# The inverse root of the query and key norms: one power on GpSimd in place of logarithm, exponential and three Newton operations

## The chip, the cores and the metric

The kernel runs on one core of a Trainium2 chip. The metric is device time in microseconds of one execution. Three runs of the kernel before gave 1486.89, 1487.9 and 1488.19 us; the median is 1487.9.

The core has five engines that work side by side, each through its own queue of instructions in order: TensorE (PE; its weight loads are shown apart as PEld), VectorE (DVE), ScalarE (ACT), GpSimd (POOL) and SyncE (SP, which here only starts DMA transfers). An instruction that waits holds everything behind it on its engine.

## The reference, cut to what matters

An attention block whose queries and keys are normalised, then a feed-forward block with a gate. The shapes: 8 batches, 12 heads, 448 tokens, 64 numbers a head; the feed-forward block has 3584 tokens, 768 inputs, 1536 hidden units.

```python
def rmsnorm(x, g):
    rms = np.sqrt(np.mean(x * x, axis=-1, keepdims=True) + 1e-06)
    return x / rms * g
q_n, k_n = (rmsnorm(q, g_q), rmsnorm(k, g_k))
scores = (1 / np.sqrt(64)) * np.matmul(q_n, k_n.transpose(0, 1, 3, 2))
attn = softmax(scores)                     # row by row
x = heads_side_by_side(np.matmul(attn, v)) # 3584 x 768
g = x @ w_gate
out = (g / (1 + np.exp(-g)) * (x @ w_val)) @ w_out
```

The change touches one thing in it: how `1 / sqrt(sum of squares + 64e-6)` is computed for each token and head of q and k. The factor sqrt(64) that turns the mean into a sum is folded into the gains.

## The kernel before, in words

The kernel holds two paths: `fast`, which ran here, and `general`, which is taken only where the gains are large and didn't run.

**Pairs.** Attention is done for two heads of one batch at a time, 48 such pairs in all. `attention(m)` adds the pieces of pair m: queries and keys come in by DMA as blocks of 32 x 32 (L728); ScalarE squares them (L754), VectorE sums the squares of each 32 numbers (L768), ScalarE copies the half sums to the partitions of the neighbouring half (L778), and VectorE adds the two halves and the small constant (L782). Then comes the inverse root (L678 to L686, below). GpSimd multiplies the keys and then the queries by it (L795), VectorE transposes both (L811), ScalarE scales the queries by the gains (L814), and TensorE makes the scores (L840). Exponentials follow on ScalarE (L855), the weighted sums on TensorE (L916), the denominators on TensorE (L947), a reciprocal on VectorE (L982), and the division (L1005, L1008, L1012).

**Inverse root.** `inverse_root` adds two pieces. The first, on ScalarE, is `rr = exp(-0.5 * ln(ss * GAIN**-2))`, two instructions on a tile of 128 x 28. It needs the table set that holds logarithm and exponential, which the planner calls mode "logarithms". The second, on VectorE, is a Newton step of three instructions on tiles of the same size. The result is larger than the true inverse root by the factor GAIN; the gains are multiplied by GAIN**-2 to take the two factors (of queries and keys) out again.

**Stages.** Twelve pairs (batches 0 and 1) are done first, while weights are loaded and converted: each of 24 parts is fetched by DMA, scaled on ScalarE (L1146, L1150), rounded on VectorE (L1168, L1174, L1180), combined on GpSimd in twelve sums (L1199, L1202), and stored back to DRAM, all as a preparation of a faster form of matrix product. Then come four blocks, each of two batches. A block has an up phase (gate and value products, L1328, with Silu on ScalarE, L1402) and a down phase (L1502). Beside the down phase of blocks 0 to 2 run the twelve attention pairs of the next two batches. Silu needs another table set than the exponential, so ScalarE loads a table (L552 and L1402 in the trace) each time it goes from one to the other.

**What sets the order.** Nothing runs in the order in which the text has it. `Order` is a planner: each piece is added with its engine, an expected time in us, a due time, the pieces it follows, the buffers it takes and uses, and a mode. `run` plays all pieces through a model of the engines, and emits at each step the piece that can start first, with ties broken by due time; a piece on GpSimd is handicapped by 0.7 us in that choice, and a change of table set on ScalarE counts 1.3 us. Pieces with `port=True` are kept from overlapping with each other between VectorE and GpSimd. `takes` names a buffer out of a ring; a piece that takes one waits for the last user of the old content. The planner's times only set the order: on the chip each instruction waits by semaphores for what it needs.

The planner's entries for the inverse root are 0.5 us on ScalarE and 0.45 us on VectorE; the buffer ring `rr` has four places, `ss` two.

Of the kernel before, what the change touches and what calls it, by code (L numbers as in the profile page):

```python
# [9 lines left out]
F32 = mybir.dt.float32  # L10
U32 = mybir.dt.uint32
I64 = mybir.dt.int64
AF = mybir.ActivationFunctionType
ALU = mybir.AluOpType
# [346 lines left out]
class Order:  # L361
# [24 lines left out]
    def add(  # L386
        self, engine, us, when, emit, after=(), takes=(), uses=(), port=False, kb=0, group=None,
        mode=None, early=None, rank=0.0, slack=0.1,
    ):
        piece = dict(  # L390
            engine=engine, us=us, when=when, emit=emit, takes=takes, port=port, kb=kb,
            group=group, mode=mode, early=early, rank=rank, slack=slack,
            after=[a for a in after if a is not None], end=None, n=len(self.pieces),
        )
        for tile_of in (*takes, *uses):
            self.users.setdefault(tile_of, []).append(piece)
        self.pieces.append(piece)
        return piece
# [79 lines left out]
def fast(  # L478
# [41 lines left out]
    nc = tc.nc  # L520
# [3 lines left out]
    P = 128  # L524
# [15 lines left out]
    const = ctx.enter_context(tc.tile_pool(name="const", bufs=1))  # L540
# [7 lines left out]
        rr=4, ws=2, **{x + str(i): 1 for x in "vw" for i in range(6)},  # L548
# [5 lines left out]
    order = Order(BUFS, dict(logarithms=load_tables))  # L554
    tiles = {}
# [10 lines left out]
    def take(name, key, shape):  # L566
        if name in ("e", "ea"):
            at = order.turn[name] % BUFS[name]
            tiles[name, key] = es[:, at] if at < BUFS["e"] else more_es[:, at - BUFS["e"]]
            return tiles[name, key]  # L570
        if name in OFTEN:
            at = OFTEN[name] + order.turn[name] % BUFS[name]
            tiles[name, key] = spare[:, ts(at, S)]
            return tiles[name, key]
        if name == "eh":
            at = order.turn["eh"] % BUFS["eh"]
            tiles[name, key] = more[:, at].rearrange("p (h q) -> p h q", h=2)
            return tiles[name, key]
        if name in WORK:
            at, size = WORK[name]  # L580
            at += order.turn[name] % BUFS[name] * size
            n = 1
            for length in shape[1:]:
                n *= length
            x = work[0 : shape[0], at : at + n]
            letters = "abcd"[: len(shape) - 1]
            x = x.rearrange(
                f"p ({' '.join(letters)}) -> p {' '.join(letters)}",
                **dict(zip(letters, shape[1:])),
            )  # L590
            tiles[name, key] = x
            return x
        pool = psum if name in ("st", "at") else sbuf
        tiles[name, key] = pool.tile(shape, F32, name=name, bufs=BUFS[name])
        return tiles[name, key]
# [33 lines left out]
    gq2 = const.tile([P, 1], F32, name="gq2")  # L629
    gk2 = const.tile([P, 1], F32, name="gk2")  # L630
    gg = const.tile([P, 1], F32, name="gg")

# [14 lines left out]
    def pair_time(m):  # L649
        if m < EARLY:  # L650
            return LEAD + m * PAIR, PAIR
        n, i = divmod(m - EARLY, EARLY)
        return block_end(n) + (i - 1) * BOTH / EARLY, BOTH / EARLY
# [10 lines left out]
    down_products = {}  # L664


    GAIN = 2.0**24

    SCALE = 2.0**8
    SPREAD = 6.0  # L670

    def inverse_root(m, sums, of, when, rank=0.0):


        def estimate():
            ss = of()
            rr = take("rr", m, list(ss.shape))
            nc.scalar.activation(rr, ss, AF.Ln, scale=GAIN**-2)  # L678
            nc.scalar.activation(rr, rr, AF.Exp, scale=-0.5)

        def improve():
            ss, rr = of(), tiles["rr", m]
            times = nc.vector.scalar_tensor_tensor
            times(ss, rr, GAIN**-2, ss, op0=ALU.mult, op1=ALU.mult)  # L684
            times(ss, ss, -0.5, rr, op0=ALU.mult, op1=ALU.mult)
            times(rr, ss, 1.5, rr, op0=ALU.add, op1=ALU.mult)  # L686

        first = order.add(
            "ACT", 0.5, when, estimate, after=[sums], uses=[("ss", m)], takes=[("rr", m)],
            mode="logarithms", rank=rank,  # L690
        )
        return order.add(
            "DVE", 0.45, when + 1.0, improve, after=[first], uses=[("ss", m), ("rr", m)],
            rank=rank,
        )

    NC = S // C
    clusters = {}
# [4 lines left out]
    def attention(m):  # L703
# [10 lines left out]
        ready = base - span  # L714
        early = m < EARLY
        rank = 60.0 if early else 0.0

        def add(*what, **more):
            return order.add(*what, rank=rank, **more)
# [37 lines left out]
        for x in range(2):  # L757
# [3 lines left out]
                    after=[loaded[x], *squares], uses=[("qk", (m, x))] + [("t", m)] * x,  # L761
                    takes=[("t", m)] * (1 - x),
# [17 lines left out]
        def both():  # L780
# [5 lines left out]
        sums = add(  # L786
            "DVE", 1.1, ready - 17.0, summed, after=squares, uses=[("t", m)], takes=[("ss", m)]
        )
        sums = add("ACT", 0.9, ready - 16.0, swap, after=[sums], uses=[("ss", m)])
        sums = add("DVE", 0.15, ready - 15.0, both, after=[sums], uses=[("ss", m)])  # L790
        rr = inverse_root(m, sums, lambda: tiles["ss", m][:, 0], ready - 14.0, rank)

        def scale(x):
            rr = tiles["rr", m][:, ts(x, NC)].rearrange("p (c one) -> p c one", one=1)
# [8 lines left out]
                uses=[("qk", (m, x)), ("t", m), ("rr", m)],  # L803
# [9 lines left out]
        def queries():  # L813
# [7 lines left out]
            uses=[("t", m)],  # L821
# [3 lines left out]
            uses=[("t", m), ("qk", (m, 0))],  # L825
# [3 lines left out]
            takes=[("QT", m)],  # L829
# [19 lines left out]
        def weights_of(j):  # L849
            return ("ea" if early else "e", (m, j)) if j < NJ - 1 else ("eh", m)  # L850
# [20 lines left out]
        for j in (3, 0, 1, 2):  # L871
            before = clusters.get((m - 2, "weighted" if j in (3, 0) else "total"))
            when = (ready + 0.3 if j in (3, 0) else base) + 0.01 * (j % 3)
# [3 lines left out]
                after=[kt, qt, staged.get(ES), before],  # L877
                uses=[("KT", m), ("QT", m)], takes=[("st", (m, j))],
# [4 lines left out]
                after=[st], uses=[("st", (m, j))],  # L883
                takes=[weights_of(j)], mode="logarithms",
            )
            if j in (1, 2) and not early:

                def more_sums(j=j):
                    if j == 1:
# [7 lines left out]
                        takes=[("sums", m)] if j == 1 else [],  # L897
# [57 lines left out]
        when = base + span * 0.8 if late else pair_time(m + 1)[0] + 0.1  # L955
        at = [("at", (m, x)) for x in range(2)]
        last = None
        for j in range(NJ):
# [3 lines left out]
                after=[*ex.values(), load_v, last, clusters.get((m - 1, "total"))],  # L962
                takes=at if j == 0 else [],
                uses=[weights_of(j), ("v", m)] + at * (j > 0),
# [6 lines left out]
            after=[last, *adds] + ([bank_read[m % 2]] if of_bank else []),  # L971
            uses=[weights_of(j) for j in range(NJ)] if early else [("sums", m)],
            takes=[] if of_bank else [den], group=("c", m + 1), mode="strips",
# [36 lines left out]
        def divide():  # L1010
# [9 lines left out]
            takes=[("rd", m)],  # L1020
        )
        if early:
            inv = add(
                "PE", 0.82, when + SPREAD, spread_by_product, after=[inv], mode="full", slack=1.0,
                uses=[("rd", m)] + ([] if of_bank else [den]),
            )
        else:
            inv = add(
                "ACT", 3.0, when + 4.5, spread, after=[inv, staged.get(SPARE)], uses=[("rd", m)],
                takes=[("inv", m)],  # L1030
# [3 lines left out]
            uses=([] if of_bank else [den]) if early else [("inv", m)], port=not early,  # L1034
# [554 lines left out]


    nc.gpsimd.memset(many, SCALE)
    nc.gpsimd.memset(halves, 0.0)
    for x in range(2):
        nc.gpsimd.memset(halves[ds(D * x, D), x], SCALE)
# [7 lines left out]
    for i in range(P // C):  # L1602
# [2 lines left out]
    gains = order.add(  # L1605
        "DVE", 0.2, 9.0,
        lambda: nc.vector.scalar_tensor_tensor(
            out=gg, in0=gq2, scalar=8.0 * GAIN**-2, in1=gk2, op0=ALU.mult, op1=ALU.mult
        ),
        early=0.0,  # L1610
    )
    for m in range(EARLY):
        attention(m)
    first = [(up_weights, i) for i in range(4 * NG)] + [(down_weights, i) for i in range(2 * NG)]
# [11 lines left out]
    for n in range(NB):  # L1626
        block(n)
        for m in range(EARLY * (n + 1), min(NM, EARLY * (n + 2))):
            attention(m)
# [4 lines left out]
def kernel(  # L1634
# [27 lines left out]
    )  # L1662
    nc.vector.tensor_scalar(out=fits, in0=top, scalar1=8.0, scalar2=None, op0=ALU.is_le)
    fast(tc, *args)
    fits = nc.values_load(fits[0:1, 0:1], min_val=0, max_val=1)
    with tc.If(fits == 0):
# [31 lines left out]
```

## Time and profile before

| what | value |
|---|---|
| median of three runs | 1487.9 us |
| span of the profiled execution (first to last instruction) | 1484.0 us |
| median less that span | 3.9 us |
| mean granted TensorE clock | 0.997 |
| scaling on GpSimd (L795), 96 instructions | 105.9 us, mean 1122 ns, median 941 ns |
| logarithm (L678) and exponential (L679) on ScalarE, 48 each | 10.7 us, 224 ns and 10.9 us, 226 ns |
| Newton step on VectorE (L684, L685, L686), 48 each | 12.0 us, 250 ns; 9.0 us, 187 ns; 10.8 us, 224 ns |
| sum of the two halves on VectorE (L782), 48 | 18.7 us, mean 389 ns, median 186 ns, longest 2083 ns |
| table loads on ScalarE | 22 of 1283 ns |

The last instructions of the profile are output transfers; the span runs from the first to the last instruction, and what lies around it (start and end of the execution) is in the time of a run, but not in the span. The profile has no time of its own for the whole execution: the profiled execution is known by its span alone, and the runs by their times.

A line of the profile names the line of the program, the engine, the operation, the tile it writes and the tiles it reads, and then the shape. Two instructions of one line with different tiles are two groups. A bracket such as `[0.55 <-ACT rr L679]` says that the engine had been idle for 0.55 us and that the end of the named instruction let it go on.

### The profile page before, as it was taken

Reading aid. Unit: us, or ns where it says so; the run is one execution under the profiler, and the core shown is the slowest. Engines: PE = TensorE matmul, PEld = TensorE weight load, DVE = VectorE, ACT = ScalarE, POOL = GpSimd, SP = SyncE. Lnnn points to the kernel's source line nnn. Section 1 sums busy time; section 2 is a strip of 40 time slices with the busy share of each in tenths; the row PEclk is TensorE's granted clock in tenths of the full one; section 3 lists DMA queues with packets and bytes.
Section 4 is the critical chain, followed back from the end, with each engine's and each line's share of the span. In section 5 each row is a group of like instructions: output and inputs, shape, how many; then the busy total and the mean of one; then the engine's idle time right before and its main releaser. Section 6 shows DMA issues by size and latency. Waiting matters only on the chain.

```text
span 1484.0 us, 19470 instructions
## 1 busy us (share of the span) xinstructions
PE 1425.0 (96%) x6672; PEld 675.4 (46%) x6672; DVE 916.0 (62%) x1405; ACT 681.5 (46%) x1366; POOL 414.1 (28%) x468
## 2 busy tenths in 40 slices
PE   5789999999999999999999999999999999999998
PEld 2334544443444455544444445554444445555553
DVE  4777887877978544355886733454786854432533
ACT  6774544437775322445767422354676532122100
POOL 2454586636444100012544200011343410000000
PEclk9999999999999999999999999999999999999999
DMA  7767999974453432533344432352353442222235
GB/s 165 158 144 236 292 308 341 296 219 90 99 115 85 113 106 71 138 103 90 74 111 110 100 117 73 106 136 77 96 119 85 90 119 89 80 98 73 83 98 107
DMA packets 415921, 193.30 MB, mean 130 GB/s; under 512 B 324164, under 2 KB 397892, under 8 KB 409668
## 3 DMA queue, kind: packets, MB, share of 16 engines
q1 hardware_dynamic: 402688, 190.35, 48.0%
q10 hardware_dynamic: 12996, 1.61, 0.7%
q8 instruction: 55, 0.90, 0.3%
q14 instruction: 54, 0.44, 0.1%
q0 software_dynamic: 128, 0.00, 0.0%
HBM read 157.29 MB, written 34.60 MB: 129 GB/s over the span
## 4 chain that ended last, share of the span: by engine, by line
PE 73%; DVE 3%; ACT 2%; issue 1%; DMA 1%; SPq 1%; ACTq 0%; DVEq 0%
PE mm L1502 22%; PE mm L1328 20%; PE at L1328 20%; PE st L840 6%; PE at L916 5%; PE st L947 1%; ACT spare L1000 1%; ACT es L855 1%; DVE rd L982 1%; DMA out_dram<-spare 0%; SPq L728 0%; DVE ss L782 0%; DMA work<-in_k_dram 0%; DVE ss L768 0%; DVE sums L866 0%
## 5 line engine op out<-in xcount | busy, mean ns | idle before, releaser
L1328 PE MATMUL mm<-xs,ws 128*128 128x448 f32 x960 | 401.2, 540 | 4.4 <-DVE spare L1276 2.2
L1328 PE MATMUL at<-xs,ws 128*128 128x448 f32 x960 | 400.6, 540 | 4.1 <-DVE v L1274 2.6
L1328 PEld LDWEIGHTS mm<-xs,ws 128*128 128x128 f32 x960 | 181.5, 190 | 185.8 <-issue 173.8
L1328 PEld LDWEIGHTS at<-xs,ws 128*128 128x128 f32 x960 | 181.9, 190 | 184.6 <-issue 172.6
L795 POOL TENSOR_TENSOR work<-work,rr 128x448 f32<-128x448 f32 x96 | 105.9, 1122 | 503.5 <-DVE rr L686 245.2
L840 PE MATMUL st<-work 64*64 64x448 f32 (+1 forms) x1536 | 155.1, 508 | 27.3 <-ACT work L814 21.2
L1502 PE MATMUL mm<-gt,ws 128*128 128x448 f32 x448 | 177.2, 545 | 0.0
L1272 DVE TENSOR_TENSOR gt<-gt,mm 128x448 f32<-128x448 f32 x64 | 39.7, 621 | 185.1 <-PE mm L1328 171.3
L1502 PE MATMUL mm<-hs,ws 128*128 128x448 f32 x384 | 152.1, 545 | 0.9 <-DVE ss L684 0.9
L855 ACT ACTIVATE es<-st 128x896 f32<-128x896 f32 x129 | 114.3, 913 | 56.1 <-PE at L916 42.8
L860 POOL TENSOR_TENSOR sums<-es 128x896 f32<-128x896 f32 x36 | 75.7, 2104 | 195.8 <-PE st L947 83.2
L1402 ACT ACTIVATE st<-gt 128x448 f32<-128x448 f32 x96 | 52.4, 547 | 163.8 <-DVE gt L1276 85.9
L1000 ACT COPY spare<-rd 32x224 f32<-32x224 f32 x288 | 108.1, 375 | 35.0 <-DVE rd L982 30.7
L1502 PEld LDWEIGHTS mm<-gt,ws 128*128 128x128 f32 x448 | 82.9, 190 | 84.2 <-issue 81.0
L916 PE MATMUL at<-es,v 64*64 64x448 f32 x1032 | 110.2, 545 | 7.2 <-ACT xs L1005 3.3
L1270 ACT COPY gt<-mm 128x448 f32<-128x448 f32 x80 | 42.5, 531 | 141.5 <-PE mm L1328 141.4
L1502 PEld LDWEIGHTS mm<-hs,ws 128*128 128x128 f32 x384 | 71.1, 190 | 72.9 <-issue 70.9
L840 PEld LDWEIGHTS st<-work 64*64 64x64 f32 x1536 | 50.9, 134 | 108.7 <-issue 38.1
L1270 ACT COPY v<-at 128x448 f32<-128x448 f32 x96 | 51.1, 532 | 83.2 <-PE at L1328 80.0
L860 POOL TENSOR_TENSOR sums<-sums,es 128x896 f32<-128x896 f32 x36 | 78.7, 2187 | 2.8
L811 DVE STREAM_TRANSPOSE work<-work 128x448 f32<-128x448 f32 x96 | 59.2, 627 | 25.2 <-POOL work L795 23.1
L916 PEld LDWEIGHTS at<-es,v 64*64 64x64 f32 x1032 | 39.7, 134 | 67.4 <-issue 57.4
(150 smaller groups left out, 1568.7 us busy)
## 6 DMA issues: line engine op xcount, KB each, us to landing
ws<-up_sides SPq DMA_DIRECT2D x32, 1024.0 KB, 4.9
ws<-down_sides SPq DMA_DIRECT2D x16, 1024.0 KB, 5.0
ws<-down_sides SPq DMA_DIRECT2D x28, 512.0 KB, 4.0
ws<-up_sides SPq DMA_DIRECT2D x16, 768.0 KB, 4.6
work<-in_q_dram SPq DMA_DIRECT2D x192, 56.0 KB, 2.4
work<-in_k_dram SPq DMA_DIRECT2D x188, 56.0 KB, 2.5
out_dram<-spare SPq DMA_DIRECT2D x168, 56.0 KB, 1.9
v<-in_v_dram SPq DMA_DIRECT2D x96, 96.0 KB, 2.5
```

The lines of the kernel that those rows point to most:

```text
L795: nc.gpsimd.tensor_tensor(out=tiles["t", m][:, x], in0=tiles["qk", (m, x)], in1=rr.to_broadcast([P, NC, C]), op=ALU.mult,)
L811: nc.vector.transpose(to, tiles["t", m][:, x].rearrange("p c f -> p (c f)"))
L840: nc.tensor.matmul(st[ds(D * x, D), h, 0:n], tiles["KT", m][rows, ds(P * j + D * of_keys, D)], tiles["QT", m][rows, ds(Q * of_queries, n)] ...
L855: nc.scalar.activation(e, tiles["st", (m, j)][:, :, 0 : S * width(j) // P], AF.Exp)
L860: nc.gpsimd.tensor_tensor(out=to, in0=tiles["e", (m, 0)] if j == 1 else to, in1=e, op=ALU.add)
L916: nc.tensor.matmul(tiles["at", (m, x)][ds(D * h, D), queries], tiles["v", m][rows, j, h], tiles["e", (m, j)][rows, h], start=j == 0, stop= ...
L1000: nc.scalar.copy(inv[ds(D * h + C * to, C), ts(x, Q)], tiles["rd", m][ds(D * h + C * x, C)])
L1270: nc.scalar.copy(to, ps)
L1272: nc.vector.tensor_tensor(out=to, in0=old, in1=ps, op=ALU.add)
L1328: nc.tensor.matmul(ps(), w[:, at, which, c], xs[:, SLOT[x], c], start=fresh and c == 0, stop=c == NC2 - 1, skip_group_check=True,)
L1402: nc.scalar.activation(take(*act, [P, 2, TB])[:, 0, 0:S], to, AF.Silu)
L1502: nc.tensor.matmul(banks[s][:, 0:S], w[:, at, s, g], where[x][:, g], start=fresh and g == 0, stop=g == NG - 1, skip_group_check=True,)
```

## The change

`inverse_root` and its two pieces go, and GAIN with them. In their place `attention` adds one piece on GpSimd: the sum raised to the power minus one half, on the same 128 x 28 tile, with the exponent read from a column of -0.5 that is spread along the row. That column is filled once at the start by a memset on GpSimd. The new piece has a planner time of 0.5 us and the due time of the old first piece, is not marked `port`, and has no table mode. The gains lose the factor GAIN**-2. The table set that is loaded for exponentials stays the same, under the same name.

```diff
+    minus_half = const.tile([P, 1], F32, name="minus_half")
...
-    GAIN = 2.0**24
...
-    def inverse_root(m, sums, of, when, rank=0.0):
-        def estimate():
-            ss = of()
-            rr = take("rr", m, list(ss.shape))
-            nc.scalar.activation(rr, ss, AF.Ln, scale=GAIN**-2)
-            nc.scalar.activation(rr, rr, AF.Exp, scale=-0.5)
-
-        def improve():
-            ss, rr = of(), tiles["rr", m]
-            times = nc.vector.scalar_tensor_tensor
-            times(ss, rr, GAIN**-2, ss, op0=ALU.mult, op1=ALU.mult)
-            times(ss, ss, -0.5, rr, op0=ALU.mult, op1=ALU.mult)
-            times(rr, ss, 1.5, rr, op0=ALU.add, op1=ALU.mult)
-
-        first = order.add(
-            "ACT", 0.5, when, estimate, after=[sums], uses=[("ss", m)], takes=[("rr", m)],
-            mode="logarithms", rank=rank,
-        )
-        return order.add(
-            "DVE", 0.45, when + 1.0, improve, after=[first], uses=[("ss", m), ("rr", m)],
-            rank=rank,
-        )
...
-        rr = inverse_root(m, sums, lambda: tiles["ss", m][:, 0], ready - 14.0, rank)
+
+        def roots():
+            nc.gpsimd.tensor_tensor(
+                out=take("rr", m, [P, 2 * NC]), in0=tiles["ss", m][:, 0],
+                in1=minus_half.to_broadcast([P, 2 * NC]), op=ALU.pow,
+            )
+
+        rr = add(
+            "POOL", 0.5, ready - 14.0, roots, after=[sums], uses=[("ss", m)], takes=[("rr", m)]
+        )
...
+    nc.gpsimd.memset(minus_half, -0.5)
...
-            out=gg, in0=gq2, scalar=8.0 * GAIN**-2, in1=gk2, op0=ALU.mult, op1=ALU.mult
+            out=gg, in0=gq2, scalar=8.0, in1=gk2, op0=ALU.mult, op1=ALU.mult
```

## The prediction

> **What bounds the kernel now.** I read the page first (busy shares, then the forty slices), then busy time by stretch, then TensorE's waits in the first 140 us, then the first 15 us instruction by instruction, because the stretches point there.
>
> ```profile
> PE 1425.0 (96%) x6672; PEld 675.4 (46%) x6672; DVE 916.0 (62%) x1405; ACT 681.5 (46%) x1366; POOL 414.1 (28%) x468
> ...
> PE   5789999999999999999999999999999999999998
> ```
>
> TensorE is busy for 1425.0 of 1484.0 us: 59.0 us are all that any change off TensorE can win. The second line says that the holes lie in the first four slices. By stretch (columns: stretch, its length, PE, PEld, DVE, ACT, POOL busy, clock, DMA share, GB/s):
>
> ```profile
> 0.00:20.00 20.00, 5.34 (x40) 1.98 (x40) 7.47 (x23) 9.18 (x22) 6.56 (x16) 1.00 0.76 146
> ...
> 40.00:60.00 20.00, 14.28 (x181) 5.95 (x179) 13.93 (x27) 13.78 (x28) 7.30 (x12) 1.00 0.68 167
> 60.00:80.00 20.00, 16.30 (x172) 6.83 (x168) 17.73 (x29) 16.77 (x33) 13.79 (x21) 1.00 0.81 190
> ...
> 140.00:320.00 180.00, 173.62 (x461) 86.54 (x460) 145.86 (x218) 81.00 (x109) 112.42 (x218) 1.00 0.98 302
> 320.00:505.00 185.00, 179.73 (x1131) 76.56 (x1129) 146.89 (x217) 119.93 (x277) 81.27 (x48) 1.00 0.46 104
> 505.00:690.00 185.00, 184.94 (x527) 92.41 (x528) 81.95 (x146) 63.81 (x122) 11.93 (x10) 1.00 0.36 102
> ```
>
> The seven stretches up to 140 us hold 105.6 us of TensorE work, so 34.4 us are idle; from 140 to 505 us 11.7; from 505 to 1400 only 5.5; in the tail from 1400 7.4. In the up phase of block 1 (505 to 690) 0.06 us are idle: nothing can be won there. What TensorE waits for up to 140 us (total us, times, longest):
>
> ```profile
> PE st L840 <- ACT work L814: 21.2, 6, 14.7
> PE at L916 <- ACT xs L1005: 3.3, 2, 2.3
> PE at L916 <- DVE xs L1008: 2.7, 2, 2.1
> PE at L916 <- ACT gt L855: 2.3, 2, 1.3
> PE mm L990 <- DVE rd L982: 2.0, 2, 1.3
> ```
>
> 14.7 of the 21.2 us are the start; the other five waits for the scaled queries (L814) hold 6.5 us. The start, in order of time (start, length, engine, line):
>
> ```profile
> 9.80 0.19 DVE L782 SCALAR_TENSOR_TENSOR ss<-ss 128x28 f32<-128x28 f32 x1 [0.95 <-ACT ss L778]
> ...
> 10.02 0.23 ACT L678 ACTIVATE rr<-ss 128x28 f32<-128x28 f32 x1 [0.25 <-DVE ss L782]
> 10.28 0.23 ACT L679 ACTIVATE rr<-rr 128x28 f32<-128x28 f32 x1
> ...
> 10.98 0.19 DVE L686 SCALAR_TENSOR_TENSOR rr<-ss,rr 128x28 f32<-128x28 f32 x1
> ...
> 11.39 1.83 POOL L795 TENSOR_TENSOR work<-work,rr 128x448 f32<-128x448 f32 x2 [7.79 <-DMA v<-in_v_dram]
> ```
>
> So from the end of the sum (9.99) to the first scaling on GpSimd (11.39) pass 1.40 us, and every one of them delays the first matmul at 14.66.
>
> **What the Trainium skill says.** GPSIMD Engine Reference, section 7, gives 4 cycles per element for a dependent fp32 chain, and section 1 a clock of 1.2 GHz; no page prices a power, and no power runs in this trace. SBUF — State Buffer, "Who interferes with whom": a VectorE instruction with two SBUF inputs and a GpSimd instruction that reads SBUF exclude each other, the later one blocks. The trace agrees: the last Newton operation (L686) has a median of 188 ns and a maximum of 1956, the scaling (L795) a median of 941 and a maximum of 2815. ScalarE: Activation LUTs, "What ACT_TABLE_LOAD costs", says about 1283 ns; the trace has 22 loads of 1283 ns.
>
> **Removed.** ScalarE: 48 × (224 + 226) ns = 21.6 us, of it 5.3 us in the first 140. VectorE: 48 × (250 + 187 + 224) ns = 31.8 us, 6.8 of it in the first 140. Table loads: in the up phases of blocks 1 and 2 five return trips (at 613, 640, 962, 976 and 996 us) load the exponential's set directly before a logarithm. Exponentials that follow at 659 us would load it anyway, so I count three to five trips gone, 6 to 10 loads, 7.7 to 12.8 us of ScalarE. All of that lies under TensorE at 184.94 of 185 us: worth nothing. The constant in the gains and one memset (about 0.1 us, before GpSimd's four short gain loads, 8 us ahead of its first use): nothing.
>
> **Added.** 48 powers on 128x28. Floor: plain sums on GpSimd take about 0.47 us on 128x128 and 0.73 on 128x256, so 2.0 ns an element and 0.21 us fixed: 0.27 us on 28. From above: with c dependent operations an element, 28 × 4 / 1.2 ns = 0.093 us each (estimate from the skill's section 7); the power replaces a logarithm and an exponential, and I take c between nothing and 30: 0.3 to 3.1 us. I take c = 15: 0.27 + 1.4 = 1.7 us. The planner believes 0.5.
>
> **Moved.** The old way from sum to scaling, read off the first seven pairs: 1.40, 1.80, 1.31, 2.36, 2.03, 1.64, 1.43 us, mean 1.71. The new way: a semaphore's 0.22 us (L686's end at 11.17 to 11.39) plus the power; the scaling follows on the same engine. Break-even is a power of 1.2 us for the first pair and 1.5 for the mean one.
> Behind the waiting power stand, on GpSimd's queue, the two scalings of its pair and the conversion's sums (L1199, L1202), for which the store of the weights' sides on SP's queue waits; later the sums of exponentials (L860), for which the denominators wait. In blocks 1 to 3 a pair has 28.3 us and GpSimd needs about 6.3 of them, so 1.7 more hide. That cover would be gone only from some 20 us a power.
>
> **Sum.** First pair: 0.22 + 1.7 − 1.40 = +0.5. The five later waits on L814, each longer by 0.22 + 1.7 − 1.71 = 0.2: +1.0. VectorE's queue up to 140 us: its transposes (L811) stand at the head waiting for GpSimd (24 waits in the run, 23.1 us). The planner errs by 1.7 − 0.5 = 1.2 us a pair where it erred by about 0.2 (0.45 for three operations that need 0.66), so 12 × 1.0 = 12 us more of such waits, against 6.8 us of work and some 3 to 4 us of waits for L679 taken away: 1 to 2 us net, say +1. Block 0's second half (5.3 us idle) and its edges: +0.5. Together +3 on the span of 1484.0, so 1487. The median of the runs stands 3.9 us above that span (1487.9), so 1491.
>
> **Rivals.**
> A short power. At 0.5 us the first pair gains 0.7, the five waits 1.0 each, and VectorE's relief takes a fraction of the 4.7 us that TensorE waits for L1008 and L982: −5, 1483. For it: the removed pieces are on the path in the only stage with room. Against it: at 44 and 58 us the queries waited behind squares (L754) whose loads were late, and a shorter root moves no DMA. It decides from a power below 0.8 us.
> A long power, 3 us: the first pair +1.8, the five waits +1.5 each, VectorE's extra waits 12 × 2.5 − 10 = 20, of which half hides: +15 with the overlap taken off, 1503. For it: no operation in this trace says that it is cheap.
> GpSimd late with the weights: its queue loses 12 × 1.2 = 14 us against the plan while it forms the weights' sides. From 140 to 320 us the DMA engines are at 0.98, so sides stored late aren't caught up, and the products of block 0 wait. If half of it arrives, +7 to +10: 1497. Against it: GpSimd stands idle for 6 to 16 of every 20 us before 140.
> No effect: the new wait ends within 0.5 us of the old one and other queues decide: 1488. That the power isn't computed where the change says can't be: it is one instruction on a named engine; only its price is open.
>
> **How the numbers follow.** What this kernel's measurement tells from no change is 0.2%, 3.0 us: faster is under 1484.9, slower over 1490.9. The forecast (1486 to 1496) has 0.45, of which 0.30 lies above 1490.9 and 0.15 within; the short power 0.18 (0.17 faster, 0.01 within); the long power 0.14; GpSimd late 0.14; no effect 0.09 within. Faster 0.17, within 0.25, slower 0.58. The range 1483 to 1506 leaves out the faster half of the short power (0.09) and the powers beyond 3.1 us (0.07); the forecast's own range is 1486 to 1496.
>
> **What would show it.** The power's mean length on GpSimd, 1.7 us. The first scaling at 11.9 and the first matmul at 15.2 us. No logarithm, 12 to 16 table loads. TensorE's idle time before 140 us at 36 to 38 instead of 34.4, and the stretches after 505 us within 1 us. It is wrong if the power takes under 0.8 or over 3 us, or if the loss or the gain lies after 505 us: then the emitted order, not the length of the chain, made it.

## The result, and the profile after

The changed kernel takes 1596.61 us (median of 4 runs, 1596.06 to 1597.97) against 1487.39 us beside it: 1.0739 times as long, 95% interval 1.0724 to 1.0754. The prediction of 1491 us, and its range up to 1506, are far below it. The page of the changed kernel, busy shares and the first lines of the slices and groups:

```profile
span 1594.7 us, 19324 instructions
...
PE 1468.6 (92%) x6672; PEld 688.4 (43%) x6672; DVE 896.1 (56%) x1261; ACT 657.3 (41%) x1264; POOL 644.1 (40%) x517
...
PE   4787889996888899999998999999998989999998
...
PEclk9898999998998999999998999999999999999999
...
L767 POOL TENSOR_TENSOR rr<-ss,minus_half 128x28 f32<-128x28 f32 x48 | 237.2, 4941 | 414.6 <-DVE ss L756 406.9
```

The last line answers the first question: one power on 128x28 takes 4.94 us in the mean, 237.2 us in all. GpSimd's busy time rose by 230 us, those of VectorE and ScalarE fell by 20 and 24. TensorE's line has holes in the attention stages too. Its 110.7 us of longer span are 43.6 us of longer busy time (1425.0 to 1468.6, for the same 6672 matmuls) and 67.1 us more idle.

The same start as before, in order of time (start, length, engine, line):

```profile
10.02 0.19 DVE L756 SCALAR_TENSOR_TENSOR ss<-ss 128x28 f32<-128x28 f32 x1 [0.95 <-ACT ss L752]
...
10.36 4.82 POOL L767 TENSOR_TENSOR rr<-ss,minus_half 128x28 f32<-128x28 f32 x1 [6.70 <-DVE gg L1591]
...
15.25 1.84 POOL L778 TENSOR_TENSOR work<-work,rr 128x448 f32<-128x448 f32 x2
...
18.53 5.38 PE L823 MATMUL st<-work 64*64 64x224 f32 x32 [18.53 <-ACT work L797]
```

From the end of the sum to the scaling pass 5.04 us where 1.40 passed before, and the first matmul starts 3.9 us later. What TensorE waits for, over the whole run (total us, times, longest; the first line is of the kernel before, the others of the changed one):

```profile
PE st L840 <- ACT es L855: 3.1, 11, 0.4
...
PE st L823 <- ACT work L797: 60.5, 13, 18.5
PE st L823 <- ACT es L838: 24.9, 25, 3.5
PE at L899 <- DVE xs L991: 5.5, 2, 5.1
PE mm L1311 <- DMA ws<-up_sides: 4.3, 1, 4.3
```

The wait for the scaled queries (L814 of the kernel before, L797 here) went from 21.2 to 60.5 us, and that for the exponentials (L855, here L838), in many short pieces, from 3.1 to 24.9. The other waits in that list are of 5.5 us at most. The scaled queries come out of VectorE's transposes, and these (L811 before, L794 here) wait for GpSimd at the head of VectorE's queue:

```profile
DVE work L811 <- POOL work L795: 23.1, 24, 2.0
DVE work L794 <- POOL work L778: 156.7, 54, 6.8
```

All that VectorE has to do behind them waits as well.

Where the time went, by stage, read off the first and last up-phase product of each block in the traces (all in us; the columns "up" and "down" are the blocks' phases; the early stage is the time up to the first up-phase product, and pairs 12 to 47 are computed in the down phases of blocks 0 to 2):

| kernel | early | up 0 | down 0 | up 1 | down 1 | up 2 | down 2 | up 3 | down 3 |
|---|---|---|---|---|---|---|---|---|---|
| before | 140.1 | 189.7 | 175.3 | 185.4 | 164.8 | 185.5 | 164.9 | 180.6 | 97.7 |
| after | 164.0 | 197.2 | 221.6 | 185.6 | 182.1 | 185.6 | 180.3 | 180.6 | 97.7 |
| difference | +23.9 | +7.5 | +46.3 | +0.2 | +17.3 | +0.1 | +15.4 | 0 | 0 |

Of the loss, 103 us lie where attention is computed and 7.5 in the up phase of block 0; the other up phases and the last down phase are as before. In busy time by stretch (stretch, length, PE, PEld, DVE, ACT, POOL, clock, DMA share, GB/s), the changed kernel's early stage, down 0, up 1 and down 1:

```profile
0.00:164.00 164.00, 114.69 (x1196) 49.61 (x1197) 85.92 (x133) 89.25 (x157) 111.46 (x99) 0.91 0.56 129
...
362.00:583.00 221.00, 187.16 (x1105) 77.88 (x1106) 137.71 (x167) 114.72 (x247) 137.48 (x60) 0.92 0.36 81
583.00:768.00 185.00, 185.00 (x528) 92.17 (x528) 78.75 (x133) 59.55 (x112) 31.17 (x14) 1.00 0.36 102
768.00:950.00 182.00, 170.49 (x1058) 73.80 (x1056) 122.91 (x152) 102.20 (x219) 104.41 (x46) 0.95 0.41 91
```

No engine is full there: GpSimd is busy for 137 of 221 us in down 0. And the granted clock of TensorE is 0.92 where it was 1.00 in the kernel before. The Trainium skill (TensorE: Matmul & The Clock Gate, "What's actually happening") has it that the array's clock is halved after an idle window of some 3.4 us. This trace agrees in kind. Its records of the granted clock hold 1.0 and 0.5 and nothing between, the halves in pieces of 3.4 us or of twice or three times that, each behind a wait of TensorE. Up to the last matmul they make 106 us in all, against 3.4 in the kernel before. In one point it differs from the page: the 3.4 us before such a piece need not be idle throughout; they held up to 2.0 us of matmuls. A score matmul of 64x448 inside a piece takes 951 ns in the median, outside 536. TensorE is busy for 87.3 us of these pieces (3.4 before), so about (87.3 − 3.4) × (1 − 536/951) = 37 of the 43.6 us of longer busy time are matmuls at half the clock (an estimate from these figures). A wait of TensorE is thus paid for a second time in slower matmuls.

### The profile page after: what moved, and what is told of

It reads as the page before. It is cut to its first block, busy times and chain, and to the rows that moved or that the text cites. A ratio compares the mean times of both kernels' runs of the same rounds, so it can differ in the third digit from the quotient of the medians.

```text
span 1594.7 us, 19324 instructions
## 1 busy us (share of the span) xinstructions
PE 1468.6 (92%) x6672; PEld 688.4 (43%) x6672; DVE 896.1 (56%) x1261; ACT 657.3 (41%) x1264; POOL 644.1 (40%) x517
## 4 chain that ended last, share of the span: by engine, by line
PE 54%; DVE 8%; issue 6%; ACT 4%; POOL 3%; SPq 2%; DMA 2%; DVEq 0%; ACTq 0%; POOLq 0%
PE mm L1311 17%; PE at L1311 17%; PE mm L1485 13%; PE st L823 3%; PE at L899 2%; ACT spare L983 2%; POOL sums L843 2%; DVE xs L1036 1%; DVE rd L965 1%; SPq L702 1%; DVE sums L849 1%; POOL work L778 1%; ACT es L838 1%; DVE work L794 1%; DVE xs L995 1%
## 5 line engine op out<-in xcount | busy, mean ns | idle before, releaser
L767 POOL TENSOR_TENSOR rr<-ss,minus_half 128x28 f32<-128x28 f32 x48 | 237.2, 4941 | 414.6 <-DVE ss L756 406.9
L823 PE MATMUL st<-work 64*64 64x448 f32 (+1 forms) x1536 | 174.8, 561 | 92.0 <-ACT work L797 60.5
L1485 PE MATMUL mm<-gt,ws 128*128 128x448 f32 x448 | 186.3, 568 | 0.0
L1485 PE MATMUL mm<-hs,ws 128*128 128x448 f32 x384 | 155.3, 556 | 0.0
L794 DVE STREAM_TRANSPOSE work<-work 128x448 f32<-128x448 f32 x96 | 60.7, 636 | 162.8 <-POOL work L778 156.7
L838 ACT ACTIVATE es<-st 128x896 f32<-128x896 f32 x129 | 114.7, 914 | 67.3 <-PE at L899 39.4
L1485 PEld LDWEIGHTS mm<-gt,ws 128*128 128x128 f32 x448 | 87.4, 200 | 93.5 <-issue 90.8
L778 POOL TENSOR_TENSOR work<-work,rr 128x448 f32<-128x448 f32 x96 | 97.1, 1030 | 3.5
```

The lines of the kernel that those rows point to most:

```text
L767: nc.gpsimd.tensor_tensor(out=take("rr", m, [P, 2 * NC]), in0=tiles["ss", m][:, 0], in1=minus_half.to_broadcast([P, 2 * NC]), op=ALU.pow,)
L778: nc.gpsimd.tensor_tensor(out=tiles["t", m][:, x], in0=tiles["qk", (m, x)], in1=rr.to_broadcast([P, NC, C]), op=ALU.mult,)
L794: nc.vector.transpose(to, tiles["t", m][:, x].rearrange("p c f -> p (c f)"))
L823: nc.tensor.matmul(st[ds(D * x, D), h, 0:n], tiles["KT", m][rows, ds(P * j + D * of_keys, D)], tiles["QT", m][rows, ds(Q * of_queries, n)] ...
L838: nc.scalar.activation(e, tiles["st", (m, j)][:, :, 0 : S * width(j) // P], AF.Exp)
L1485: nc.tensor.matmul(banks[s][:, 0:S], w[:, at, s, g], where[x][:, g], start=fresh and g == 0, stop=g == NG - 1, skip_group_check=True,)
```

## The experiments

Two theories stood at the start: **length** (a power takes 4.8 us, and that alone makes the loss) and **order** (moving the root from two engines to a third made the planner emit another order, and that order is worse). A third came up between them: the order is bad because the planner was told 0.5 us.

**A short product in the power's place.**

```diff
-                in1=minus_half.to_broadcast([P, 2 * NC]), op=ALU.pow,
+                in1=minus_half.to_broadcast([P, 2 * NC]), op=ALU.mult,
...
-    nc.gpsimd.memset(minus_half, -0.5)
+    nc.gpsimd.memset(minus_half, 2.0**-9)
```

> The changed kernel with the power replaced by a plain product of the same shape (the sum times 2^-9, from a column filled with that constant); every engine has the same instructions in the same order. It leaves out the root: norms are only roughly right. Theory length (the 4.8 us that a power takes make the loss): the product takes about 0.3 us and the time falls to 1480-1492, with GpSimd's busy time about 215 us lower. Theory order (the pieces that moved to GpSimd changed the emitted order, and that order is the loss): it stays at 1560 or more.

1487.64 us (20 runs), 1.0005 times before, interval 0.9998 to 1.0011. GpSimd's groups of this run:

```profile
L767 POOL TENSOR_TENSOR rr<-ss,minus_half 128x28 f32<-128x28 f32 x48 | 18.8, 391 | 452.3 <-DVE ss L756 427.8 <-DMA work<-in_k_dram 9.5 <-DVE gg L1591 6.7
```

With the same instructions in the same order on every engine, 4.94 us become 0.39 and the whole loss goes. Order on its own, as the cause, is out. The run also prices the other side of the change: 53 us of work taken from ScalarE and VectorE, six table loads fewer, and a root that costs next to nothing win nothing in the sum. By stage it is less quiet: early 134.0 (6.1 us less than before), up 0 198.3 (8.6 more), down 0 179.8 (4.5 more), down 1 and 2 162.3 each (2.5 less). So gains of 11 us and losses of 13 cancel, and the 7.5 us that the changed kernel loses in up 0 do not come from the power's length: they are there without it. The prediction's rival "a short power" (−5 us) has the early stage right and not the whole.

**The power's price by itself.** A kernel that runs nothing but the instruction, four times each.

> None of the reference's work: the output is filled with zeros, and GpSimd runs each of twelve instructions four times in a row with nothing beside it: the power on 1, 7, 14, 28, 56 and 112 columns of 128 rows, on 28 columns with the exponent in a full tile, with exponent 2, and on 64, 16 and 4 rows; a product on 28 columns. Theory vector (each step works on all rows of a core at once): time goes with the columns at 0.17 us each, and 4, 16, 64 and 128 rows cost the same. Theory row by row: 4 rows cost about a quarter of 16. If the broadcast of the exponent is what is slow, the full tile is under half; if the root is slow and not the power in general, exponent 2 is under half.

Groups of that run (busy us in all, mean ns of one):

```profile
L54 POOL TENSOR_TENSOR pow<-x,half 128x56 f32<-128x56 f32 x4 | 37.0, 9258 | 0.0
L54 POOL TENSOR_TENSOR full<-x,full 128x28 f32<-128x28 f32 x4 | 19.1, 4788 | 0.0
L54 POOL TENSOR_TENSOR pow<-x,half 128x28 f32<-128x28 f32 x4 | 19.1, 4783 | 0.0
L54 POOL TENSOR_TENSOR square<-x,two 128x28 f32<-128x28 f32 x4 | 19.1, 4776 | 0.0
...
L54 POOL TENSOR_TENSOR rows<-x,half 4x28 f32<-4x28 f32 x4 | 19.1, 4774 | 0.0
...
L54 POOL TENSOR_TENSOR pow<-x,half 128x7 f32<-128x7 f32 x4 | 6.0, 1492 | 0.0
L54 POOL TENSOR_TENSOR pow<-x,half 128x1 f32<-128x1 f32 x4 | 2.2, 558 | 0.0
L54 POOL TENSOR_TENSOR times<-x,half 128x28 f32<-128x28 f32 x4 | 0.9, 232 | 2.2 <-DVE x L49 2.2
```

The time goes with the columns: (9258 − 558) / 55 = 158 ns each, and some 0.4 us fixed. Rows, the broadcast of the exponent, and the exponent itself make no difference. The product of the same shape takes 232 ns: a power costs twenty times that. The vector theory holds.

**The loss against the length.** In the changed kernel's order, with the planner's 0.5 us, the power on 14 or on 7 of the 28 columns and a product on the others (the diff is of the first; in the second the split is at column 7):

```diff
+            for x, by, op in ((1, minus_half, ALU.pow), (0, small, ALU.mult)):
+                nc.gpsimd.tensor_tensor(
+                    out=rr[:, ts(x, NC)], in0=ss[:, ts(x, NC)],
+                    in1=by.to_broadcast([P, NC]), op=op,
+                )
```

> The changed kernel, same order, with the power on the keys' 14 columns and a product on the queries' 14 (the queries' root is left out). GpSimd's part is then about 2.4 + 0.25 us in place of 4.8. Linear in length from the two ends (0.3 us: 1487.6, 4.8 us: 1596.6): 1543 to 1548. If a slack of 1.5 us a pair covers the first part, as the prediction had it: below 1530. If the prediction's own slope of 6.5 us for each us held: 1496.

> The changed kernel, same order and the planner's 0.5 us, with the power on 7 of the 28 columns and a product on the other 21 (three quarters of the roots are left out). Measured alone, 7 columns take 1.5 us; with the product about 1.75, which is the length that the prediction took for the whole power. If only the price was wrong and the prediction's sum holds at its own length: 1488 to 1494. If the loss is linear from 0.4 us (1487.6) over 3.1 us (1516) : 1500 to 1504. If it goes with the length beyond a slack of some 2 us: 1485 to 1490.

| mean length on GpSimd, both instructions, us | time, us | slope from the row above, us per us |
|---|---|---|
| 0.39 (product alone) | 1487.64 | |
| 1.96 (7 columns) | 1499.84 | 7.8 |
| 3.13 (14 columns) | 1516.14 | 13.9 |
| 4.94 (28 columns) | 1596.61 | 44.5 |

The ratios are 1.0075 (1.005 to 1.010) for 7 columns and 1.0203 (1.0181 to 1.0226) for 14. The five runs of 7 columns fall in two heaps, 1493 and 1500, so its slope lies between 3 and 8. The lower heap is inside what was expected if only the price was wrong, the upper one at the edge of the straight line between its neighbours; the runs do not decide between the two. Over all four lengths the curve bends upward: it is neither a straight line (1543 to 1548 for 14 columns) nor the prediction's slope of 6.5 (1496) beyond 2 us, and there is no slack that covers the first 2 us. By stage, as differences from the kernel before (the trace of 7 columns is of a run at 1493), with the whole wait of VectorE's transposes for GpSimd (23.1 before), all in us:

| power on | early | up 0 | down 0 | down 1 | down 2 | transposes' wait |
|---|---|---|---|---|---|---|
| no column (short product) | −6.1 | +8.6 | +4.5 | −2.5 | −2.6 | 11.4 |
| 7 columns | −7.0 | +7.2 | +9.2 | −0.8 | −0.9 | 54.1 |
| 14 columns | −0.9 | +7.9 | +22.6 | +1.0 | +0.1 | 79.9 |
| 28 columns (after) | +23.9 | +7.5 | +46.3 | +17.3 | +15.4 | 156.7 |

Down 0 pays first, then the early stage, and the two later down phases only beyond 3 us. Up 0 does not answer to the length at all.

**Half of the pairs.** The first 12 pairs with logarithm, exponential and Newton step and the later 36 with the power, and the reverse.

```diff
+        if early:
+            first = add(
+                "ACT", 0.5, ready - 14.0, estimate, after=[sums], uses=[("ss", m)],
+                takes=[("rr", m)], mode="logarithms",
+            )
+            rr = add(
+                "DVE", 0.45, ready - 13.0, improve, after=[first], uses=[("ss", m), ("rr", m)]
+            )
+        else:
...
```

> The first 12 pairs with logarithm, exponential and Newton step (without the factor GAIN), the other 36 with the power. By the stages of the two profiles the early stage and the up phase of block 0 lost 31 us and the three later attention phases 80. If the losses are local to their stages: 1487 + 75 to 85 = 1562 to 1572. If the late start in the early stage is what feeds the loss in the first attention phase (46 of the 80): 1525 to 1540.

> The reverse: the power in the first 12 pairs only. Losses local to their stages: 1487 + 25 to 35 = 1512 to 1522. If the early stage drags the first attention phase with it: 1530 to 1560.

1566.30 us (1.0547, 1.0522 to 1.0572) and 1518.76 us (1.0225, 1.0202 to 1.0247). The losses, 79 and 32 us, add up to the 109 of the changed kernel within 2 us: they are local. With the early stage left as it was, down 0 still takes 219.5 us.

**The planner told the truth.**

```diff
-            "POOL", 0.5, ready - 14.0, roots, after=[sums], uses=[("ss", m)], takes=[("rr", m)]
+            "POOL", 4.85, ready - 14.0, roots, after=[sums], uses=[("ss", m)], takes=[("rr", m)]
```

> The changed kernel with the planner's time of the power put at 4.85 us in place of 0.5, so that the order is made for the true length. Theory length alone (GpSimd's time and the longer chain): within 15 us of 1596. Theory mis-planning (an order made for 0.5 us puts other work behind a GpSimd that is late): at least half of the 109 us comes back, 1500 to 1545. I hold 1540 the likeliest.

1526.94 us (1.0270, 1.0247 to 1.0293): 70 of the 109 us come back with the same powers (mean 4.99 us). By stage: early 162.6, up 0 188.6, down 0 182.0, down 1 and 2 173.9 and 172.1. So in the down phases planning recovers 56 of 79 us and in up 0 all of the 7.5, in the early stage nearly nothing. The transposes' wait falls from 156.7 to 37.9 us. The same edit with the power in the later pairs only:

> As the run with the power in the last 36 pairs only, with the planner's time of the power at 4.85 us. Losses local to stages: the three attention phases keep the 23 us that they lose in the fully planned run and the early stage is back at 140, so 1487 + 20 to 26 = 1507 to 1513. If planning only moves the loss into the early stage: 1530 or more. If the power hides wholly once it is planned and the early stage no longer feeds delays into it: 1487 to 1493.

1512.62 us (1.0176, 1.0151 to 1.0201): the stages stay local again, early 142.5, down phases 184.1, 172.3, 170.1. And half a power, planned at 3.0 us:

> The run with the power on the keys' 14 columns alone (the queries' root is left out), with the planner's time at 3.0 us in place of 0.5. If planning brings back as much of it as of the full power (69 of 109 us): 1516 becomes 1494 to 1500. If half a power fits into the slack of a pair once it is planned: 1484 to 1491. If at this length only the chain counts: 1510 to 1520.

1497.39 us (1.0067, 1.0051 to 1.0082), where it had been 1516 unplanned. The down phases are then within 4 us of the kernel before (178.8, 162.8, 163.6); what is left is early (149.8).

**Chain or queue.** The root as a short product, and a power of full length behind the second scaling of the pair, written to a tile that nobody reads.

```diff
-                in1=minus_half.to_broadcast([P, 2 * NC]), op=ALU.pow,
+                in1=small.to_broadcast([P, 2 * NC]), op=ALU.mult,
...
+            if x == 0:
+                nc.gpsimd.tensor_tensor(
+                    out=unused, in0=many[:, 0 : 2 * NC],
+                    in1=minus_half.to_broadcast([P, 2 * NC]), op=ALU.pow,
+                )
```

> The changed kernel, same order, with the root as a short product (so the root is left out) and a full-length power to a tile that nobody reads, on GpSimd directly behind the second scaling of each pair: GpSimd has the same work, but the pair's own chain is without it. Theory chain (the loss is the longer way from sums to scores): 1487 to 1510. Theory queue (the loss is what stands behind the power on GpSimd): 1560 to 1600, as in the changed kernel. By the early stage alone: chain 134 to 142 us, queue 155 to 165.

1538.45 us (1.0349, 1.0328 to 1.0370): neither theory as it stood. By stage, with the short product as the zero:

| stage | short product | power beside the chain | power in the chain (after) |
|---|---|---|---|
| early | 134.0 | 143.3 | 164.0 |
| down 0 | 179.8 | 193.2 | 221.6 |
| down 1 | 162.3 | 179.7 | 182.1 |
| down 2 | 162.3 | 178.1 | 180.3 |

In the early stage and in down 0 a third of the loss (9 of 30, 13 of 42) is there with the pair's own chain kept short; the rest needs the power in the chain, where the transposes wait for it (156.7 us in the changed kernel, 27.9 with the power beside the chain). A pair's longer chain and the work held up behind the waiting transposes come together there; no run tells them apart. In down 1 and 2 the power beside the chain makes 17.4 of 19.8 and 15.8 of 18.0 us: there the time that it takes on GpSimd is nearly all that is needed. What stands behind it can be seen at one place of the changed kernel's trace (GpSimd alone, in order of time):

```profile
1196.95 6.51 POOL L767 TENSOR_TENSOR rr<-ss,minus_half 128x28 f32<-128x28 f32 x1 [6.90 <-DVE ss L756]
1203.54 1.84 POOL L778 TENSOR_TENSOR work<-work,rr 128x448 f32<-128x448 f32 x2
1205.34 2.09 POOL L843 TENSOR_TENSOR sums<-es 128x896 f32<-128x896 f32 x1
1207.51 2.08 POOL L843 TENSOR_TENSOR sums<-sums,es 128x896 f32<-128x896 f32 x1
```

GpSimd waits 6.9 us with the power at its head, then needs 6.5 for it, and only then scales the pair's keys and queries and sums the exponentials of another pair. The wait at the head is no loss by itself: with the short product it is longer than in the changed kernel, and nothing is lost (the short product first):

```profile
POOL rr L767 <- DVE ss L756: 427.8, 33, 114.8
...
POOL rr L767 <- DVE ss L756: 406.9, 35, 114.8
```

Nor do these runs show that the loss reaches TensorE by way of the sums: in down 1 its own waits are mostly for exponentials (6.3 us in seven waits) and for scaled queries (4.0 us in one). In the planned order the sums go ahead of the scalings at some places. The trace of the fully planned kernel, at a like place:

```profile
1169.60 4.79 POOL L767 TENSOR_TENSOR rr<-ss,minus_half 128x28 f32<-128x28 f32 x1 [6.05 <-DVE ss L756]
1174.36 2.07 POOL L843 TENSOR_TENSOR sums<-es 128x896 f32<-128x896 f32 x1
1176.51 2.08 POOL L843 TENSOR_TENSOR sums<-sums,es 128x896 f32<-128x896 f32 x1
1178.55 2.60 POOL L778 TENSOR_TENSOR work<-work,rr 128x448 f32<-128x448 f32 x2
```

Planning the power beside the chain should then clear the queue:

> The run with the power behind the second scaling, not read by anyone (the root is left out), with the planner's time of that scaling raised by 4.8 us. What stands behind the power on GpSimd was the whole loss in the two later attention phases (+16 us each) and a third of it in the first. If an order made for the true length clears the queue: 1487 to 1497. If GpSimd's time is short whatever the order: 1520 to 1540.

It did so only where it was the queue: down 1 and 2 fell to 166.7 each, 2 us above before, but the whole took 1542.28 us (1.0369, 1.0342 to 1.0395), because the early stage rose to 176.4. TensorE's longest wait there is for GpSimd's sums in the conversion of weights:

```profile
PE mm L1317 <- POOL work L1191: 20.4, 1, 20.4
```

So GpSimd has room for the powers in down 1 and 2 once the order is made for them. In down 0 (190.7, 15 us above before) and beside the weights in the early stage none of the orders tried for the full power had it.

**A cheaper root without GpSimd.** The kernel before with the Newton step left out.

```diff
-        return order.add(
-            "DVE", 0.45, when + 1.0, improve, after=[first], uses=[("ss", m), ("rr", m)],
-            rank=rank,
-        )
+        return first
```

> The kernel before with logarithm and exponential alone: the three Newton operations on VectorE are left out, so the roots are less exact. A root on the path that is 0.8 us shorter and 32 us less work on VectorE, without GpSimd: if there is anything to win from a cheaper root, it is here. From the short product (1487.6, no gain): within 1484 to 1491. If the gain that the short product had in the early stage (6 us) comes without its loss in block 0: 1479 to 1482.

1500.05 us (1.0087, 1.0072 to 1.0102): a miss. 32 us of work less, a shorter chain, and 13 us slower, of them 7 in the early stage and 9 in up 0. The instructions that are left are the same but for the table loads, of which the new order has 26 in place of 22. So an order of its own can cost 13 us in this kernel; why this one does is open. No run of this study is faster than the kernel before.

## Why the prediction was wrong

**The price of the power** is the step that failed: "I take c = 15: 0.27 + 1.4 = 1.7 us", with 3.1 as the upper end. Measured are 4.78 alone and 4.94 in the kernel, so c would be (4.78 − 0.27) / 0.093 = 48. The upper end was a guess about how many operations a power has, set between two figures that say nothing of it; a bound that rests on a guess is no bound.

**The sum at its own length** was off as well, in its places more than in its size. The run with 7 columns (1.96 us) lost 12 us, 5 to 13 in its single runs, where the sum had 3 for 1.7 us. Its terms in the early stage came out nearly as forecast (the trace is of a 1493 run): TensorE's first wait was 15.3 us (14.7 and 0.5 more forecast), and the transposes' wait in that stage 16.6 us against 2.5 (12 more forecast). But the stage as a whole gained 7 us, because the order and the work taken away gained 6 there with the short product too, and 16 us were lost in up 0 and down 0, where the sum had 0.5. At 3.1 us the loss is 30 us where the rival "a long power" had 15.

**The cover in the down phases** was mis-read: "a pair has 28.3 us and GpSimd needs about 6.3 of them", and the cover "would be gone only from some 20 us a power". In block 0 all twelve powers ran in the down phase (in blocks 1 and 2 eight of twelve, four in the up phase before it), so a pair had 175.3 / 12 = 14.6 us there, not 28.3; with the power GpSimd needs about 6.3 + 4.9 = 11.2 of those. That would still fit, and in the changed kernel GpSimd was free for 84 of the 221 us of down 0. What the prediction left out is that the power delays others there as well: VectorE's transposes, which it had counted in the early stage alone, wait for GpSimd for 33.8 us in down 0 and 17.4 and 17.7 in down 1 and 2, where it had been 2.7 and twice 3.6. A free share says nothing of engines that work in order. 79 of the 109 us are lost in these phases.

**The planner's error** was named (1.2 us a pair) but costed only for VectorE's transposes in the early stage. Its true size is 4.4 us a pair, and an order made for the true length takes 70 of the 109 us back.

**TensorE's clock** wasn't in the sum at all: idle time was counted once. 43.6 us of longer matmuls came on top of 67.1 us of idle time.

**The rival "GpSimd late with the weights"** was right as a mechanism for one order: with the power beside the chain and planned, TensorE waits 20.4 us for GpSimd's sums there. In the planned kernel it waits 12.2 us for a transfer of the weights' sides; that GpSimd made it late is not shown. In the changed kernel that wait is 4.3 us, so it is not where most is lost.

**What held.** The sign, in part by luck: at the prediction's own length the loss lies in up 0 and down 0 and not where it was summed. The first pair as the exposed one: the first matmul moved by 3.9 us for a power 3.1 us longer than assumed (15.2 plus 3.1 makes 18.3, measured 18.53). The work taken from ScalarE and VectorE is worth nothing in the sum: shown by the short product, 1.0005, though there gains and losses cancel. Table loads went from 22 to 16, the upper end of what was expected. The up phases of blocks 1 to 3 moved by at most 0.2 us.

## What to carry to other kernels

Before an operation is moved to an engine where the profile has no instance of it, measure that one operation alone: a run of four instructions would have given 4.8 us, against the prediction's break-even of 1.2 to 1.5. Ask of the new place not how busy the engine is but which other engines will stand waiting for the new instruction, and what stands behind it and behind them in their queues. And where an order is made from a table of durations, a wrong entry can cost more than the duration itself: here 70 of 109 us came back with the right one.

## What the runs showed of the hardware

A power on GpSimd costs 158 ns a column whatever the rows (4 or 128) and whatever the exponent (−0.5 or 2), where a product of the same shape takes 232 ns for all 28 columns. The SBUF lock that the Trainium skill describes (SBUF — State Buffer, "Who interferes with whom") shows for the power in one direction only. The one at 1196.95 us took 6.51 us, with a VectorE operation of two SBUF inputs (L1036) under way from 1196.79 for 2.02 us; the median is 4.80. The other way round nothing is held up: the same operation, begun 1.92 us into the power at 794.96 us, took the same 2.02 us. TensorE's granted clock fell from 0.997 to 0.965 in the mean, in pieces of 3.4 us at half the clock behind waits of a few us.
